# Linear attention ahead of two feed-forward stages: q, k, v laid out with token groups on partitions, and conversions re-timed

## The chip, the cores and the metric

The kernel runs on one core of a Trainium2 chip. The metric is the device time of one execution in microseconds (us). The engines are TensorE (PE in the profile; PEld is its weight load), VectorE (DVE), ScalarE (ACT), GpSimd (POOL) and SyncE (SP), which issues the transfers; the core's 16 DMA engines move the data.

## What is computed

```python
kv  = einsum('bhsd,bhse->bhde', k, v)            # 4 batches, 8 heads, 576 tokens, head size 64
out = einsum('bhsd,bhde->bhse', q, kv)
x   = out / sqrt(mean(out**2) + 1e-6) * g_norm   # then as 2304 tokens x 512
h   = x @ w_in;  g = h * clip(h + 3, 0, 6) / 6   # 512 -> 2048
x   = g @ w_out                                  # 2048 -> 512
out = sum over 4 experts of p_e * (relu(x @ w1[e]) @ w2[e])
```

All inputs and outputs are float32. The large products are made from a high and a low part of each factor (`xH`, `xL`, `gH`, `gL`, and `w[:, h, 0]`, `w[:, h, 1]` for the weights), three products for one.

## The kernel before

**Three stretches.** The attention fills roughly the first 73 us, the first feed-forward (`step`, `ff_in`, `ff_out`) comes next, and the four experts (`quad`, `outs`) take the rest. The change lies in the attention and in what is woven into it; the order of instructions on PE, DVE and ACT behind the attention is the same in both kernels.

**The attention's items.** There are `NHB` = 8 items: one batch and half of its heads, that is `HH` = 4 heads of 576 tokens. `att_load(i)` loads q, k and v of item i, 576 KB each. A head's tokens are numbered s*9 + j with 64 values of s and 9 of j (`CP` = 64, `CJ` = 9). Before, the partition is (head's parity x, s): one load fills all 128 partitions, and each partition gets runs of 9*64 floats, 2304 bytes. `att_q` transposes q on PE and ACT copies it out of PSUM, `att_kv` sums k-transposed times v over the 9 values of j (36 matmuls over 64 rows each), `att_out` multiplies q by that, `att_rms` forms the norm on DVE and ACT, and `att_x` transposes the result and writes its high and low part.

**Order.** In the attention the order on PE, DVE and ACT is the order in which the code stands (`manual_schedule`). Step i of the loop runs `att_load(i + 2)`, `att_out(i)`, `att_q(i + 1)`, `att_rms(i)`, `att_kv(i + 1)`, one half of a first feed-forward product (`ff_mm` at even i, `ff_in(..., later=True)` at odd i, from i = 2), `att_x(i - 1)` and then `conv(SLOTS[i])`. Tiles for two items exist, so the loads of item i + 2 reuse those of item i, and wait until PE has read them. SP issues all loads, one after the other.

**Weights of the first feed-forward.** `load_raw` loads one raw half tile (512 KB): h = 0 is a piece of `w_in`, h = 1 one of `w_out`; there are three buffers. `convert` is a generator that turns it into the two parts on ACT, DVE and for the first three half tiles GpSimd (L161, L164); each `next` is a slot, mostly one DVE instruction. `conv(k)` runs k slots. A finished half tile calls `load_raw` for the next.

**Low part of an item's product.** `ff_in` forms `gL` = r - `gH` on DVE (L360).

Of the kernel before, what the change touches and what calls it, by code (L numbers as in the profile page):

```python
# [17 lines left out]
def kernel(  # L18
# [28 lines left out]
    CP = P // 2  # L47
    CJ = S // CP
    CB = TB // CP
    HH = H // 2  # L50
    NP = HH // 2
# [30 lines left out]
    psa = ctx.enter_context(tc.tile_pool(name="psa", bufs=1, space=bass.MemoryType.PSUM))  # L82
# [4 lines left out]
    psx = attps.enter_context(tc.tile_pool(name="psx", bufs=1, space=bass.MemoryType.PSUM))  # L87
# [9 lines left out]
    ident = const.tile([P, P], F32, name="ident")  # L97
# [3 lines left out]
    dp = const.tile([P, B, CJ, E], F32, name="dp")  # L101
# [71 lines left out]
    st = {}  # L173
    natile = [0]

    def att_load(i):
# [12 lines left out]


    half = [slice(x * D, (x + 1) * D) for x in range(2)]
    identx = ident.rearrange("p (x s) -> p x s", x=2)
    GB = TB // D
    ppA = psp.tile([P, TB], F32, name="ppA")
    ppB = psp.tile([P, 2 * TB], F32, name="ppB")
# [1 line left out]
    def group(g):  # L197
        t, o = (ppA, g) if g < GB else (ppB, g - GB)
        return t[:, o * D:(o + 1) * D]
# [3 lines left out]
    def att_q(i):  # L203

        t = st[i]
        qT = wp.tile([P, (CJ + 1) * P], F32, tag=f"w{i % 2}", name="qT")
        t["qm"] = qm = qT[:, :2 * TB].rearrange("p (r x j s) -> p r x j s", r=NP, x=2, j=CJ // 2)
        t["q8"] = q8 = qT[:D, 2 * TB:].rearrange("p (r x s) -> p r x s", r=NP, x=2)
        pq = [pool.tile([P, 2, CJ // 2, CP], F32, tag=tag, name="pq") for pool, tag in ((psx, "x"), (psa, "a1"))]
        t["kvp"] = kvp = psk.tile([P, NP, TB], F32, tag="k", name="kvp")  # L210
        p8 = kvp[:D, :, D:D + P].rearrange("p r (x s) -> p r x s", x=2)
        for r in range(NP):
            for j in range(CJ // 2):
                nc.tensor.transpose(  # L214
                    pq[r][:, :, j, :], t["q"][:, r, 2 * j:2 * j + 2, :].rearrange("p j d -> p (j d)"), identx)
            nc.tensor.transpose(p8[:, r], t["q"][:, r, CJ - 1, :], identx)
        return [
            lambda r=r: nc.scalar.activation(
                out=qm[:, r].rearrange("p x j s -> p (x j s)"), in_=pq[r].rearrange("p x j s -> p (x j s)"),
                func=AF.Copy)  # L220
            for r in range(NP)] + [
            lambda: nc.scalar.activation(
                out=q8.rearrange("p r x s -> p r (x s)"), in_=kvp[:D, :, D:D + P], func=AF.Copy)]

    def att_kv(i):


        t = st[i]
        kvp = t["kvp"]
        for j in range(CJ):  # L230
            for x in range(2):
                for r in range(NP):
                    nc.tensor.matmul(  # L233
                        kvp[half[x ^ r], r, :D], lhsT=t["k"][half[x], r, j, :], rhs=t["v"][half[x], r, j, :],
                        start=(j == 0), stop=(j == CJ - 1))
        nc.scalar.activation(out=kvd[i % 2][:, 0], in_=kvp[:, :, :D], func=AF.Copy)
        for y in range(2):
            nc.scalar.activation(out=kvd[i % 2][half[y], 1], in_=kvp[half[1 - y], :, :D], func=AF.Copy)

    GA = CJ - 1  # L240

    def att_out(i):

        t = st[i]
        kv = kvd[i % 2]
        for jj in range(CJ // 4):
            for r in range(NP):
                for x in range(2):
                    for y, c in ((0, 0), (1, 1), (0, 1), (1, 0)):
                        g = (2 * y + jj) * HH + 2 * r + x  # L250
                        nc.tensor.matmul(
                            group(g)[half[c]], lhsT=t["qm"][half[y], r, x, 2 * jj + c, :],
                            rhs=kv[half[y], x ^ r ^ y, r], start=True, stop=True)
        for x in range(2):
            for r in range(NP):
                g = 2 * GA + x
                nc.tensor.matmul(
                    group(g)[half[r]], lhsT=t["q8"][:, r, x, :], rhs=kv[half[0], x ^ r, r],
                    start=True, stop=True)
# [87 lines left out]
    def ff_in(u, t, f, later=False, cs=(0, 1, 2, 3)):  # L347
        n = BLK[t][1]
        ff_mm(u, t, f, cs)
        ph = ph_t.pop((u, t, f))  # L350
        gH = gp.tile([P, TB], F32R, tag="gH", name="gH")[:, :n]
        gL = gp.tile([P, TB], F32R, tag="gL", name="gL")[:, :n]
        r = rp.tile([P, TB], F32, tag="r", name="r")[:, :n]
        gt[u, t, f] = gH, gL
        parts = [
            lambda: nc.scalar.activation(out=r, in_=ph, func=AF.Relu, bias=three[:, 0:1]),  # L356
            lambda: nc.vector.scalar_tensor_tensor(  # L357
                out=r, in0=r, scalar=6.0, in1=ph, op0=ALU.min, op1=ALU.mult),
            lambda: nc.scalar.activation(out=gH, in_=r, func=AF.Copy),
            lambda: nc.vector.tensor_tensor(out=gL, in0=r, in1=gH.bitcast(F32), op=ALU.subtract),  # L360
        ]
        if later:
            return parts
        for x in parts:
            x()
# [56 lines left out]
    start = {}  # L422
# [51 lines left out]

    nc.scalar.activation(out=gcol, in_=three, func=AF.Sqrt)
    att_load(1)
    load_raw()
    nc.sync.dma_start(out=gcol[0:D, :], in_=g_norm.rearrange("(p o) -> p o", o=1))
    nc.sync.dma_start(out=gcol[D:2 * D, :], in_=g_norm.rearrange("(p o) -> p o", o=1))
    SLOTS = {0: 8, 1: 2, 2: 3, 3: 0, 4: 3, 5: 1, 6: 3, 7: 0}  # L480
    nop = lambda: None
    engines = {mybir.EngineType.PE, mybir.EngineType.Activation, mybir.EngineType.DVE}
    with tc.manual_schedule(engines=engines):
# [97 lines left out]
        for y in range(2):  # L581
            h = half[y]
            for jp in range(2):
                j = slice(2 * y + jp, CJ - 1, 4)
                nc.vector.tensor_tensor(
                    out=prob[h, :B * HH].rearrange("p (b a) e -> p b a e", b=B)[:, :, 2 * jp:2 * jp + 2],
                    in0=dp[h, :, j], in1=psum_e[h, :, j].unsqueeze(3).to_broadcast([D, B, 2, E]), op=ALU.mult)
            nc.vector.tensor_tensor(
                out=prob[h, B * HH:], in0=dp[h, y::2, CJ - 1],
                in1=psum_e[h, y::2, CJ - 1:].to_broadcast([D, 2, E]), op=ALU.mult)  # L590

    N3 = start[NU1 - 1, 0] + 3 * UF[NU1 - 1]
    for n in range(NB, N3 + 1):
# [147 lines left out]
    def finish(p, e, i, ps):  # L741
        n = rows[p][i]
        pe = prob[:, n, e:e + 1]
        if e == 0:
            z = (p * NI2 + i) % 10
            acc2[i] = gp.tile([P, TB], F32, tag=("gH", "gL")[z % 2], name="acc2") if z < 8 else rp.tile(
                [P, TB], F32, tag="r", name="acc2")
            nc.vector.tensor_scalar(out=acc2[i], in0=ps, scalar1=pe, scalar2=None, op0=ALU.mult)
        else:
            nc.vector.scalar_tensor_tensor(  # L750
                out=acc2[i], in0=ps, scalar=pe, in1=acc2[i], op0=ALU.mult, op1=ALU.add)
        if e == E - 1:
            for y in range(2):
                if n < B * HH:
                    b, a = divmod(n, HH)
                    j = 4 * (a % 2) + a // 2 + 2 * y
                else:
                    b, j = 2 * (n - B * HH) + y, CJ - 1
# [141 lines left out]
```

## Time and profile before

| | |
|---|---|
| median of 3 runs | 1217.32 us (1217.02 to 1217.51) |
| profiled execution | 1218.32 us |
| its span on the core | 1216.5 us |
| PE busy | 1195.3 us, 98% |
| DVE, ACT, POOL busy | 770.1, 581.7, 8.9 us |
| DMA, mean over the span | 72 GB/s |

A span is the time from the core's first to its last instruction; the execution lasts 1.8 us longer. Shares over the whole span say little about the attention, which is 6% of it, so that stretch has to be read by itself. Of an instruction the profile gives its start, its duration, and what ended the idle time before it. The DMA share is the part of the 16 engines' time in which they had a packet in hand.

### The profile page before, as it was taken

The numbers are of one execution on the slowest core, as the hardware profiler recorded it, in microseconds if no ns is written. First come the engines' busy times: TensorE is split into PE (matmuls) and PEld (weight loads), VectorE is DVE, ScalarE is ACT, GpSimd is POOL, SyncE is SP. The second block draws the span as 40 slices with busy tenths as digits, with TensorE's granted clock in tenths as the row PEclk, the third lists the DMA queues.
The fourth block names the chain that finished last, engine by engine and source line by source line (L and its number), as shares of the span: only waits on it lengthen the run. The fifth ranks groups of instructions, "written<-read, shape, count | busy, mean of one in ns | idle before, by whom it ended". The sixth has DMA issues, their size and how long they took to land.

```text
span 1216.5 us, 17419 instructions
## 1 busy us (share of the span) xinstructions
PE 1195.3 (98%) x6999; PEld 1053.8 (87%) x6999; DVE 770.1 (63%) x1455; ACT 581.7 (48%) x1116; POOL 8.9 (1%) x16
## 2 busy tenths in 40 slices
PE   7899999999999999999999999999999999999997
PEld 6787888888888889999999989999999899999996
DVE  5889999953633844565656585656565856565652
ACT  5766554622322434444444554444445644444441
POOL 2000000000000000000000000000000000000000
PEclk9999999999999999999999999999999999999999
DMA  9612222300200002121111131122221422222202
GB/s 354 223 36 70 87 87 70 95 10 1 70 1 1 1 20 84 70 70 69 69 61 61 62 113 70 70 70 70 70 70 70 121 70 70 70 70 70 70 1 52
DMA packets 59345, 87.18 MB, mean 72 GB/s; under 512 B 3712, under 2 KB 36480, under 8 KB 59264
## 3 DMA queue, kind: packets, MB, share of 16 engines
q1 hardware_dynamic: 59264, 86.07, 21.1%
q8 instruction: 55, 0.90, 0.3%
q14 instruction: 26, 0.21, 0.0%
HBM read 81.34 MB, written 4.72 MB: 71 GB/s over the span
## 4 chain that ended last, share of the span: by engine, by line
PE 93%; DVE 3%; DMA 2%; ACT 1%; issue 1%; SPq 0%; DVEq 0%; ACTq 0%
PE po L734 32%; PE po L378 15%; PE qa L767 14%; PE qb L767 14%; PE ph L343 5%; PE ph L344 5%; PE ph L345 5%; DMA vin<-in_v_dram 1%; DMA qin<-in_q_dram 1%; DVE acc L750 1%; DVE xl L301 1%; PE kvp L233 1%; DVE r L357 0%; PE pq L214 0%; DVE ssq L264 0%
## 5 line engine op out<-in xcount | busy, mean ns | idle before, releaser
L734 PE MATMUL po<-wout,g 128*128 128x512 f32 x1728 | 402.1, 390 | 0.0
L734 PEld LDWEIGHTS po<-wout,g 128*128 128x128 f32 x1728 | 323.6, 188 | 65.4
L767 PE MATMUL qb<-xs,win 128*128 128x384 f32 x1008 | 203.5, 336 | 1.2 <-ACT us L808 1.2
L767 PE MATMUL qa<-xs,win 128*128 128x384 f32 x1008 | 203.1, 336 | 0.0
L378 PE MATMUL po<-gH,w 128*128 128x512 f32 (+1 forms) x632 | 191.8, 368 | 0.0
L767 PEld LDWEIGHTS qb<-xs,win 128*128 128x128 f32 x1008 | 178.1, 188 | 3.8 <-ACT us L808 1.8
L767 PEld LDWEIGHTS qa<-xs,win 128*128 128x128 f32 x1008 | 178.3, 188 | 2.2 <-ACT us L808 0.2
L641 DVE TENSOR_TENSOR wout<-raw,wout 128x512 fp32r<-128x512 f32 x96 | 62.2, 688 | 171.4 <-ACT wout L640 171.4
L640 ACT ACTIVATE wout<-raw 128x512 fp32r<-128x512 f32 x96 | 55.4, 625 | 227.0 <-PE po L734 227.0
L378 PEld LDWEIGHTS po<-gH,w 128*128 128x128 f32 x632 | 115.7, 188 | 20.5 <-ACT acc L392 0.6
L343 PE MATMUL ph<-xh,w 128*128 128x512 f32 (+1 forms) x320 | 119.2, 373 | 1.2 <-DVE r L357 1.2
L344 PE MATMUL ph<-xl,w 128*128 128x512 f32 (+1 forms) x320 | 118.4, 370 | 0.0
L345 PE MATMUL ph<-xh,w 128*128 128x512 f32 (+1 forms) x320 | 118.2, 370 | 0.0
L356 ACT ACTIVATE r<-ph,three 128x512 f32<-128x512 f32 (+1 forms) x80 | 51.6, 645 | 138.3 <-PE ph L345 138.2
L378 PE MATMUL po<-gL,w 128*128 128x512 f32 (+1 forms) x316 | 116.3, 368 | 0.0
L357 DVE SCALAR_TENSOR_TENSOR r<-r,ph 128x512 f32<-128x512 f32 (+1 forms) x80 | 50.5, 631 | 91.0 <-ACT r L356 90.8
L797 DVE SCALAR_TENSOR_TENSOR g<-sums,g 128x384 fp32r<-128x384 f32 x96 | 53.6, 559 | 81.4 <-ACT g L794 81.4
L794 ACT ACTIVATE g<-cs 128x384 fp32r<-128x384 f32 x96 | 50.4, 525 | 63.3 <-DVE cs L810 54.4
L640 ACT ACTIVATE win<-sums 128x512 fp32r<-128x512 f32 x96 | 60.6, 632 | 40.1 <-DVE sums L653 37.6
L343 PEld LDWEIGHTS ph<-xh,w 128*128 128x128 f32 x320 | 60.6, 189 | 12.4 <-DVE r L357 1.6
L797 DVE SCALAR_TENSOR_TENSOR g<-cs,g 128x384 fp32r<-128x384 f32 x96 | 53.2, 554 | 27.2 <-ACT g L794 27.2
L345 PEld LDWEIGHTS ph<-xh,w 128*128 128x128 f32 x320 | 60.6, 189 | 10.3
(129 smaller groups left out, 1260.7 us busy)
## 6 DMA issues: line engine op xcount, KB each, us to landing
raw<-in_moe_w_dram SPq DMA_DIRECT2D x96, 512.0 KB, 4.1
raw<-in_moe_w_in_dram SPq DMA_DIRECT2D x16, 512.0 KB, 3.7
raw<-in_moe_w_out_dram SPq DMA_DIRECT2D x16, 512.0 KB, 3.5
qin<-in_q_dram SPq DMA_DIRECT2D x8, 576.0 KB, 7.1
kin<-in_k_dram SPq DMA_DIRECT2D x8, 576.0 KB, 8.3
vin<-in_v_dram SPq DMA_DIRECT2D x8, 576.0 KB, 9.4
out_dram<-acc SPq DMA_DIRECT2D x36, 128.0 KB, 2.3
dp<-in_moe_domain_probs_dram SPq DMA_DIRECT2D x2, 36.0 KB, 8.4
```

The source lines that it names most:

```text
L343: nc.tensor.matmul(ph, lhsT=w[:, 0, c, :], rhs=xH[t][:, c, :], start=(c == 0), stop=False)
L344: nc.tensor.matmul(ph, lhsT=w[:, 0, c, :], rhs=xL[t][:, c, :], start=False, stop=False)
L345: nc.tensor.matmul(ph, lhsT=w[:, 1, c, :], rhs=xH[t][:, c, :], start=False, stop=(c == KD - 1))
L356: lambda: nc.scalar.activation(out=r, in_=ph, func=AF.Relu, bias=three[:, 0:1]),
L357: lambda: nc.vector.scalar_tensor_tensor(out=r, in0=r, scalar=6.0, in1=ph, op0=ALU.min, op1=ALU.mult),
L378: nc.tensor.matmul(po_t[u, t][o], lhsT=lhsT, rhs=rhs, start=(f == 0 and m == 0), stop=(f == UF[u] - 1 and m == 2))
L640: nc.scalar.activation(out=dst[0], in_=src, func=AF.Copy)
L641: nc.vector.tensor_tensor(out=dst[1], in0=src, in1=dst[0].bitcast(F32), op=ALU.subtract)
L734: nc.tensor.matmul(ps[i], lhsT=lhsT, rhs=w[:, f, y], start=(j == 0 and f == 0 and m == 0), stop=(j == FP - 1 and f == 1 and m == 2))
L767: nc.tensor.matmul(bank, lhsT=w[:, wy, AOP[m], c], rhs=xs[m][:, xy, c], start=first and n == 0, stop=n == 5, skip_group_check=True)
L794: nc.scalar.activation(out=g[f][:, 0, t], in_=src, func=func)
L797: nc.vector.scalar_tensor_tensor(out=g[f][:, 1, t], in0=src, scalar=0.0, in1=g[f][:, 0, t].bitcast(F32), op0=ALU.max, op1=ALU.subtract)
```

## The change

**Layout.** The partition is now (token group y, s): group 0 holds j = 0 to 4, group 1 holds j = 5 to 8, and each of the four heads has its own place in the row. One tensor of an item comes in two loads, one per group, each into 64 partitions, with runs of 1280 and 1024 bytes. `att_kv` then sums over 128 rows for four values of j and over 64 rows for the fifth: 20 matmuls for 36. `att_q` has 12 transposes for 10, `att_out` has as many matmuls as before. `att_q`, `att_out`, the routing weights `prob` and the rows that `finish` stores only follow the new numbering.

**Raw loads and slots.** The `load_raw` ahead of the loop is gone, and the calls in the loop are at i = 0, 3 and 5 for i = 1 and 3. `SLOTS` has the same sum, 20, with fewer slots early and more in steps 2 to 6.

**Low part.** `ff_in(..., later=True)` forms `gL` on GpSimd; that is three instructions of 80.

```diff
     def att_load(i):
...
-            t[nm] = pool.tile([P, NP, CJ, D], F32, tag=tag, name=f"{nm}in")
-            nc.sync.dma_start(
-                out=t[nm].rearrange("p r j d -> p r (j d)"),
-                in_=src[b, hf * HH:(hf + 1) * HH].rearrange("(r x) (s j) d -> (x s) r (j d)", x=2, j=CJ),
-            )
+            t[nm] = pool.tile([P, HH, JG, D], F32, tag=tag, name=f"{nm}in")
+            for y in range(2):
+                j = slice(y * JG, min((y + 1) * JG, CJ))
+                nc.sync.dma_start(
+                    out=t[nm][half[y], :, :j.stop - j.start].rearrange("p h j d -> p h (j d)"),
+                    in_=src[b, hf * HH:(hf + 1) * HH].rearrange("h (s j) d -> s h j d", j=CJ)[:, :, j]
+                    .rearrange("s h j d -> s h (j d)"))
...
     def att_kv(i):
...
-        for j in range(CJ):
-            for x in range(2):
-                for r in range(NP):
+        for j in range(JG):
+            rows = slice(0, P) if j < JP else half[0]
+            for r in range(NP):
+                for x in range(2):
                     nc.tensor.matmul(
-                        kvp[half[x ^ r], r, :D], lhsT=t["k"][half[x], r, j, :], rhs=t["v"][half[x], r, j, :],
-                        start=(j == 0), stop=(j == CJ - 1))
+                        kvp[half[x], r, :D], lhsT=t["k"][rows, 2 * r + x, j, :], rhs=t["v"][rows, 2 * r + x, j, :],
+                        start=(j == 0), stop=(j == JP))
...
-            lambda: nc.vector.tensor_tensor(out=gL, in0=r, in1=gH.bitcast(F32), op=ALU.subtract),
+            lambda: (nc.gpsimd if later else nc.vector).tensor_tensor(out=gL, in0=r, in1=gH.bitcast(F32), op=ALU.subtract),
...
     att_load(1)
-    load_raw()
...
-    SLOTS = {0: 8, 1: 2, 2: 3, 3: 0, 4: 3, 5: 1, 6: 3, 7: 0}
+    SLOTS = {0: 2, 1: 0, 2: 4, 3: 2, 4: 5, 5: 3, 6: 4, 7: 0}
...
-            if i in (1, 3):
+            if i in (0, 3, 5):
                 load_raw()
```

`JG` is 5, `JP` is 4, and `half[y]` is the upper or lower 64 partitions.

On SP, the kernel's first loads before (items 0 and 1 and the first two raw half tiles, by name of the tile and tensor, with partitions x runs x floats of a run):

```order
L184 DMA qin<-in_q_dram 128x2x576
L184 DMA kin<-in_k_dram 128x2x576
L184 DMA vin<-in_v_dram 128x2x576
L126 DMA raw<-in_moe_w_in_dram 128x4x256
L184 DMA qin<-in_q_dram 128x2x576
L184 DMA kin<-in_k_dram 128x2x576
L184 DMA vin<-in_v_dram 128x2x576
L130 DMA raw<-in_moe_w_out_dram 128x1024
```

and the start of the same place with the change:

```order
L190 DMA qin<-in_q_dram 64x4x320
L190 DMA qin<-in_q_dram 64x4x256
L190 DMA kin<-in_k_dram 64x4x320
L190 DMA kin<-in_k_dram 64x4x256
L190 DMA vin<-in_v_dram 64x4x320
L190 DMA vin<-in_v_dram 64x4x256
L126 DMA raw<-in_moe_w_in_dram 128x4x256
L190 DMA qin<-in_q_dram 64x4x320
L190 DMA qin<-in_q_dram 64x4x256
```

Each load is now two, of 64 partitions each, and the raw `w_out` tile stands no longer behind item 1 but behind item 2.

On SP, the last loads of the attention with the change (end of item 6, a raw `w_out` tile, item 7, the next raw `w_in` tile):

```order
L190 DMA vin<-in_v_dram 64x4x320
L190 DMA vin<-in_v_dram 64x4x256
L130 DMA raw<-in_moe_w_out_dram 128x1024
L190 DMA qin<-in_q_dram 64x4x320
L190 DMA qin<-in_q_dram 64x4x256
L190 DMA kin<-in_k_dram 64x4x320
L190 DMA kin<-in_k_dram 64x4x256
L190 DMA vin<-in_v_dram 64x4x320
L190 DMA vin<-in_v_dram 64x4x256
L126 DMA raw<-in_moe_w_in_dram 128x4x256
```

Ahead of item 7 stand four raw tiles in all; before there were five, all of them ahead of item 6.

On DVE, between the products of the low parts `xl` of steps 3 and 4 before (`gL` is the low part of an item, `ssq` the sums of squares):

```order
L301 SCALAR_TENSOR_TENSOR xl_123<-px,gcol,xh_118 128x512 x2
L301 SCALAR_TENSOR_TENSOR xl_126<-kvp,gcol,xh_121 128x2x64
L360 TENSOR_TENSOR gL<-r,gH 128x512
L264 TENSOR_REDUCE ssq<-xt 128x8
L264 TENSOR_REDUCE ssq<-xt 128x10
```

and with the change:

```order
L306 SCALAR_TENSOR_TENSOR xl_123<-px,gcol,xh_118 128x512 x2
L306 SCALAR_TENSOR_TENSOR xl_126<-kvp,gcol,xh_121 128x2x64
L158 TENSOR_SCALAR x<-a 128x512
L269 TENSOR_REDUCE ssq<-xt 128x8
L269 TENSOR_REDUCE ssq<-xt 128x10
```

The `gL` is gone from DVE, and a slot of a conversion stands in its place; steps 4 and 5 get two further slots each.

## Rows read from the trace of the kernel before

**Rows 1.** The page's 40 equal slices of the span.

```profile
DMA  9612222300200002121111131122221422222202
GB/s 354 223 36 70 87 87 70 95 10 1 70 1 1 1 20 84 70 70 69 69 61 61 62 113 70 70 70 70 70 70 70 121 70 70 70 70 70 70 1 52
```

**Rows 2.** Busy time by stretch: PE, PEld, DVE, ACT, POOL, granted clock, DMA share, GB/s.

```profile
2.00:22.00 20.00, 16.34 (x343) 13.14 (x345) 9.70 (x20) 10.54 (x26) 3.78 (x3) 1.00 1.01 369
22.00:42.00 20.00, 14.84 (x408) 12.50 (x409) 15.05 (x34) 13.27 (x32) 1.30 (x2) 0.97 0.92 329
42.00:58.00 16.00, 15.93 (x351) 13.35 (x349) 12.40 (x27) 11.60 (x29) 2.56 (x2) 0.93 0.70 220
58.00:76.00 18.00, 16.97 (x292) 14.14 (x291) 16.93 (x35) 14.98 (x31) 0.00 (x0) 1.00 0.01 2
76.00:100.00 24.00, 22.81 (x109) 18.14 (x109) 19.18 (x38) 16.95 (x33) 0.00 (x0) 1.00 0.22 67
```

**Rows 3.** The chain of waits, 0 to 130 us: start, duration, what.

```profile
10.95 10.83 DMA vin<-in_v_dram
21.91 1.31 PE kvp L233 x72
...
37.68 2.89 issue
...
61.94 1.21 PE kvp L233 x72
...
73.91 1.39 PE po L546 x6
```

**Rows 4.** PE's timeline around item 7: start, duration, instruction, what ended idle time.

```profile
61.09 0.30 PE L216 MATMUL kvp<-ident,qin 128*64 128x128 f32 x1 [0.20 <-DVE xl L301]
...
61.87 1.28 PE L233 MATMUL kvp<-vin,kin 64*64 64x64 f32 x72
```

**Rows 5.** SP's issues in the attention: the first, and item 7's last.

```profile
0.73 0.44 SPq L184 DMA_DIRECT2D qin<-in_q_dram  x1
...
49.65 0.46 SPq L184 DMA_DIRECT2D vin<-in_v_dram  x1
```

**Rows 6.** The page's transfers: issue, count, KB each, us to landing.

```profile
raw<-in_moe_w_in_dram SPq DMA_DIRECT2D x16, 512.0 KB, 3.7
...
dp<-in_moe_domain_probs_dram SPq DMA_DIRECT2D x2, 36.0 KB, 8.4
```

**Rows 7.** Transfers from 18 to 22 us, nearly all q, k, v.

```profile
DMA packets 744, 1.62 MB, mean 405 GB/s; under 512 B 47, under 2 KB 47, under 8 KB 743
```

**Rows 8.** Transfers from 7 to 8 us, nearly all runs of 1 KB.

```profile
DMA packets 327, 0.34 MB, mean 339 GB/s; under 512 B 6, under 2 KB 319, under 8 KB 327
```

**Rows 9.** Transfers from 1206 to 1216 us: the last stores, of 64 partitions each.

```profile
DMA packets 960, 1.57 MB, mean 157 GB/s; under 512 B 192, under 2 KB 192, under 8 KB 960
...
q1 hardware_dynamic: 960, 1.57, 67.6%
...
out_dram<-acc SPq DMA_DIRECT2D x12, 128.0 KB, 2.3
```

**Rows 10.** Busy time inside the stretch of the stores, columns as in rows 2.

```profile
1208.00:1214.00 6.00, 1.01 (x5) 0.51 (x3) 1.80 (x3) 0.00 (x0) 0.00 (x0) 0.80 0.88 205
```

**Rows 11.** Busy time around the stretch at half clock, columns as in rows 2.

```profile
35.00:40.80 5.80, 2.91 (x103) 2.56 (x95) 5.37 (x13) 3.33 (x7) 0.00 (x0) 1.00 0.92 306
40.80:44.20 3.40, 3.40 (x22) 2.60 (x15) 0.00 (x0) 1.37 (x5) 0.00 (x0) 0.50 0.62 179
```

**Rows 12.** DVE's timeline, steps 3 to 4.

```profile
46.97 0.68 DVE L360 TENSOR_TENSOR gL<-r,gH 128x512 fp32r<-128x512 f32 x1
...
53.56 0.68 DVE L155 SCALAR_TENSOR_TENSOR a<-raw,x 128x512 uint32<-128x512 uint32 x1
54.27 0.43 DVE L158 TENSOR_SCALAR x<-a 128x512 uint32<-128x512 uint32 x1
```

**Rows 13.** GpSimd's timeline, one conversion.

```profile
54.84 1.27 POOL L161 TENSOR_TENSOR r<-r,x 128x512 f32<-128x512 f32 x1 [31.46 <-ACT qT L218]
```

More of the change, by code (lines that the diff above doesn't have):

```diff
@@ L174 @@
     natile = [0]
+    JG, JP = CJ // 2 + 1, CJ // 2
+    half = [slice(x * D, (x + 1) * D) for x in range(2)]
     def att_load(i):
@@ L182, in att_load @@
             pool, tag = (accp, "acc") if m < 5 else (wp, f"w{m - 1}")
-            t[nm] = pool.tile([P, NP, CJ, D], F32, tag=tag, name=f"{nm}in")
-            nc.sync.dma_start(
-                out=t[nm].rearrange("p r j d -> p r (j d)"),
-                in_=src[b, hf * HH:(hf + 1) * HH].rearrange("(r x) (s j) d -> (x s) r (j d)", x=2, j=CJ),
-            )
+            t[nm] = pool.tile([P, HH, JG, D], F32, tag=tag, name=f"{nm}in")
[5 more added lines that the diff above has]
+                    .rearrange("s h j d -> s h (j d)"))
         st[i] = t
-    half = [slice(x * D, (x + 1) * D) for x in range(2)]
-    identx = ident.rearrange("p (x s) -> p x s", x=2)
     GB = TB // D
@@ L206, in att_q @@
         qT = wp.tile([P, (CJ + 1) * P], F32, tag=f"w{i % 2}", name="qT")
-        t["qm"] = qm = qT[:, :2 * TB].rearrange("p (r x j s) -> p r x j s", r=NP, x=2, j=CJ // 2)
-        t["q8"] = q8 = qT[:D, 2 * TB:].rearrange("p (r x s) -> p r x s", r=NP, x=2)
-        pq = [pool.tile([P, 2, CJ // 2, CP], F32, tag=tag, name="pq") for pool, tag in ((psx, "x"), (psa, "a1"))]
+        t["qm"] = qm = qT[:, :2 * TB].rearrange("p (h j t) -> p h j t", h=HH, j=JP // 2)
+        t["q8"] = q8 = qT[:D, 2 * TB:].rearrange("p (h s) -> p h s", h=HH)
+        pq = [pool.tile([P, 2, JP // 2, P], F32, tag=tag, name="pq") for pool, tag in ((psx, "x"), (psa, "a1"))]
         t["kvp"] = kvp = psk.tile([P, NP, TB], F32, tag="k", name="kvp")
         p8 = kvp[:D, :, D:D + P].rearrange("p r (x s) -> p r x s", x=2)
-        for r in range(NP):
-            for j in range(CJ // 2):
+        for h in range(HH):
+            r, x = divmod(h, 2)
+            for j in range(JP // 2):
                 nc.tensor.transpose(
-                    pq[r][:, :, j, :], t["q"][:, r, 2 * j:2 * j + 2, :].rearrange("p j d -> p (j d)"), identx)
-            nc.tensor.transpose(p8[:, r], t["q"][:, r, CJ - 1, :], identx)
+                    pq[r][:, x, j, :], t["q"][:, h, 2 * j:2 * j + 2, :].rearrange("p j d -> p (j d)"), ident)
+            nc.tensor.transpose(p8[:, r, x], t["q"][half[0], h, JP, :], ident[half[0], :D])
         return [
             lambda r=r: nc.scalar.activation(
-                out=qm[:, r].rearrange("p x j s -> p (x j s)"), in_=pq[r].rearrange("p x j s -> p (x j s)"),
-                func=AF.Copy)
+                out=qm[:, 2 * r:2 * r + 2].rearrange("p x j t -> p (x j t)"),
+                in_=pq[r].rearrange("p x j t -> p (x j t)"), func=AF.Copy)
             for r in range(NP)] + [
             lambda: nc.scalar.activation(
-                out=q8.rearrange("p r x s -> p r (x s)"), in_=kvp[:D, :, D:D + P], func=AF.Copy)]
+                out=q8.rearrange("p (r x) s -> p r (x s)", x=2), in_=kvp[:D, :, D:D + P], func=AF.Copy)]
     def att_kv(i):
@@ L245, in att_out @@
         kv = kvd[i % 2]
-        for jj in range(CJ // 4):
+        for jj in range(JP // 2):
             for r in range(NP):
@@ L249, in att_out @@
                     for y, c in ((0, 0), (1, 1), (0, 1), (1, 0)):
-                        g = (2 * y + jj) * HH + 2 * r + x
                         nc.tensor.matmul(
-                            group(g)[half[c]], lhsT=t["qm"][half[y], r, x, 2 * jj + c, :],
-                            rhs=kv[half[y], x ^ r ^ y, r], start=True, stop=True)
+                            group((2 * y + jj) * HH + 2 * r + x)[half[c]],
+                            lhsT=t["qm"][half[y], 2 * r + x, jj, half[c]],
+                            rhs=kv[half[y], x ^ y, r], start=True, stop=True)
         for x in range(2):
             for r in range(NP):
-                g = 2 * GA + x
                 nc.tensor.matmul(
-                    group(g)[half[r]], lhsT=t["q8"][:, r, x, :], rhs=kv[half[0], x ^ r, r],
+                    group(2 * GA + x)[half[r]], lhsT=t["q8"][:, 2 * r + x, :], rhs=kv[half[0], x, r],
                     start=True, stop=True)
@@ L583 @@
             for jp in range(2):
-                j = slice(2 * y + jp, CJ - 1, 4)
+                j = slice(JG * y + jp, JG * y + JP, 2)
                 nc.vector.tensor_tensor(
-                    out=prob[h, :B * HH].rearrange("p (b a) e -> p b a e", b=B)[:, :, 2 * jp:2 * jp + 2],
+                    out=prob[h, :B * HH].rearrange("p (b z a) e -> p b z a e", b=B, z=2)[:, :, jp],
                     in0=dp[h, :, j], in1=psum_e[h, :, j].unsqueeze(3).to_broadcast([D, B, 2, E]), op=ALU.mult)
             nc.vector.tensor_tensor(
-                out=prob[h, B * HH:], in0=dp[h, y::2, CJ - 1],
-                in1=psum_e[h, y::2, CJ - 1:].to_broadcast([D, 2, E]), op=ALU.mult)
+                out=prob[h, B * HH:], in0=dp[h, y::2, JP],
+                in1=psum_e[h, y::2, JP:JP + 1].to_broadcast([D, 2, E]), op=ALU.mult)
     N3 = start[NU1 - 1, 0] + 3 * UF[NU1 - 1]
@@ L755, in finish @@
                     b, a = divmod(n, HH)
-                    j = 4 * (a % 2) + a // 2 + 2 * y
+                    j = 2 * (a % 2) + a // 2 + JG * y
                 else:
-                    b, j = 2 * (n - B * HH) + y, CJ - 1
+                    b, j = 2 * (n - B * HH) + y, JP
                 nc.sync.dma_start(
```

1 line of the change is left out of this document (removed).

## The prediction, made before the run

> **What bounds the kernel now.** I read the slices of the page first: behind the third slice the transfers need a small part of the time, while in the first two the 16 DMA engines are busy for nearly all of it [rows 1]. So the busy time by stretch comes next, for the attention alone. From 2 to 22 us the engines have a packet in hand all the time and PE's 16.34 us hold much filling work; from 22 to 42 us it is still 0.92; from 58 us on nothing is loaded and DVE is busy for 16.93 of 18 us [rows 2]. The reader is to see two regimes: loads set the pace at first, the chain through PE, ACT and DVE later. The chain of waits says the same: 10.83 us of it are v of the third item, which ends in that item's kv product [rows 3]. Late, PE reaches item 7's q and kv work after a wait for DVE [rows 4], and item 7's last load had been issued at 49.65 us [rows 5], 12 us ahead. Behind item 7's kv product (its end at 61.94 + 1.21 = 63.15 us) the same instructions follow in both kernels but for one `gL`, so the end moves with that moment. That is the quantity to forecast.
>
> **The loads, part by part.** An item is 3 x 576 KB = 1.77 MB. Now it runs at 405 GB/s [rows 7], 4.37 us per item. The change alters two things.
>
> Shorter runs: runs of 1 KB go at 339 GB/s [rows 8], those of 2304 bytes at 405. Per engine (a sixteenth) that is 48.3 ns for 1024 bytes and 91.0 ns for 2304; a straight line between them gives 56.9 ns for 1280. A pair of new runs takes 105.2 ns for the 91.0 of an old one: 5.05 us per item, 0.68 more.
>
> 64 partitions per load: the only loads of that kind in the trace are small (the routing weights, 36 KB in runs of 144 bytes [rows 6]) and tell nothing of pace, but the stores of the result are of that kind too. The last twelve, 128 KB each, alternate between the two halves exactly as the new loads would, and move 205 GB/s while the engines hold packets for 0.88 of the time [rows 10]. Their packets are long: 67.6% of 16 x 10 us are 108 us, over 768 packets of 2 KB (the 192 short ones left at nothing) 141 ns each [rows 9], where the line above gives 82 ns. Engines that are busy and still slow share something, and following a load of the lower half by one of the upper did not free it. I carry this over to the loads. The bounds are 205 GB/s and 205/0.88 = 233 GB/s, if the gaps could be filled at the same pace; I take 212, since an engine's gap is also when another runs faster, so filled gaps give less than their share.
>
> [...]
>
> **The sum.** Eight items at 212 GB/s are 8 x 8.34 = 66.7 us. Four raw half tiles lie ahead of item 7's last piece, one behind item 0: two of 1 KB runs (524 KB at 339 GB/s = 1.55 us) and two of longer ones (at 405, 1.30 us), 5.7 us. A lone raw tile lands after 3.7 us [rows 6], 1.55 of them moving, so 2.2 us are latency. The first issue is at 0.73 us [rows 5]. Item 7's v then lands at 0.73 + 2.2 + 66.7 + 5.7 = 75.3 us, if the queue never empties: k and v of item i + 2 wait for PE's reading of item i, and item i + 1 (8.3 us of transfer) is then still on its way. SP issues twice as often, six loads of some 0.46 us [rows 5] in those 8.3 us, so it keeps up. It lets eight loads be under way and waits for the first of them before the ninth; with loads half as large these are 8 x 288 KB = 2.4 MB, 11 us at the forecast's pace, so that wait too leaves the engines with work.
>
> The kv product after it: 40 matmul passes instead of 72. In 1.21 us [rows 3] 72 of 64 rows went in four quarters of the array. If the rate of issue is the limit, 40 take 0.67 us; if twice as many rows take twice as long, 1.34. I take 1.0. It ends at 76.3 us, 13.2 later than before.
>
> [...] With 8.3 us per item PE idles more, so the same can meet the products behind item 7: nothing to 1.7 us for one such stretch, 2 us as the bound; I take 1.0. The sum is 14.2 us later: 1218.3 + 14.2 = 1232.5 us for the profiled execution. That execution is 1.0 us above the median of the runs, so the median comes out at **1231.5 us**.
>
> **What lies under this.** The transposes (12 for 10), the moved slots and the low part cost nothing here: each step waits some 8.3 us for its loads, and the steps before needed about 7 (42 to 63 us for three). Without that cover, three slots more in steps 4 and 5 are two DVE instructions of 0.43 and one of 0.68 us [rows 12], and others on ACT; against them stand two `gL` of 0.68 us [rows 12] off DVE, which take GpSimd 1.27 us each by its nearest row [rows 13]. Nothing waits for those in the same step. The third `gL` lies in the last step, and its reader stands behind another product of the first feed-forward; cover again. The raw `w_out` tile's new place is worth 1.3 us for item 2 and nothing at item 7, where the total counts; there one raw tile fewer stands ahead, and it is in the sum.
>
> **The rivals.** *Faster: the stores' pace is a matter of stores.* If loads into 64 partitions only pay for shorter runs, items 0 to 2 land 3 x 0.68 = 2.0 us later, less 1.3 for the `w_out` tile; from item 3 on kv is up to 0.54 us shorter per item, 2.7 in all, and 1.4 us of `gL` leave DVE's chain against 0.9 us of slots: 0.7 - 2.7 - 0.5 = -2.5, so 1214.8 us. PE's unexplained pause in the middle of a kv product, 2.89 us [rows 3], may shrink with fewer instructions: down to 1211.9. For it: stores end in DRAM, loads don't. Against it: the engines' packets were held up, not the queue. [...]
>
> *Same: gain and loss cancel.* As above, but kv stays near 1.21 us (twice the rows, half the count) and the `gL` had been in DVE's idle time: 0.7 + 0.9 - 0.7 = about +1, at most 1219.
>
> *Slower by little: conversions.* Loads at full pace and a DVE that carries the extra slots of steps 4 to 6 (0.9 us), ACT with two more copies of one 128x512 tile at 0.65 us (DVE's row for that size is 0.68 [rows 12]), the first items later by 0.7, kv and `gL` without a gain: 0.9 + 1.3 + 0.7 = 2.9, 1220.2 us. It decides if DVE, not the loads, ends the waits in steps 4 and 5, and if `gL` had stood in idle time.
>
> **How the numbers follow.** The forecast's own range: at 233 GB/s the items take 60.7 us, with kv at 0.67 and no half clock 1224.2; at 205, with kv at 1.34 and 2 us of clock, 1235.2, and one more for a queue that empties now and then, 1236. It gets 0.78, the faster rival 0.12, the same 0.05, the small loss 0.05. A measurement of this kernel tells 0.2%, 2.4 us, from no change. Faster by more: 0.12, since most of that rival's spread lies at or below 1214.9. Same: 0.05. Slower: 0.78 and the small loss of 2.9 us: 0.83. The range 1220 to 1237 leaves out the fast cases and little else.
>
> **What would show it.** Right: transfers of q, k, v at 200 to 235 GB/s with the engines busy, until beyond 70 us; PE's waits in every step end with v's load; item 7's kv product ends near 76 us. Wrong: those loads near 350 GB/s, or the steps from 42 us on still waiting for DVE. If loads run at 350 GB/s, the forecast falls as a whole.

## The result, and the profile of the changed kernel

The changed kernel takes 1230.84 us (median of 4 runs, 1229.60 to 1231.11), the kernel before on the same chip 1217.41 us (median of 4 runs): a ratio of 1.0105, 95% interval 1.0088 to 1.0123, so 13.4 us slower. The forecast was 1231.5 us. The profiled execution spans 1229.3 us, 12.8 more than before.

The page of the changed kernel, its 40 slices:

```profile
PEclk8999999999999999999999999999999999999999
DMA  9942222210100001221111142212112321112102
GB/s 222 240 109 70 86 70 85 91 47 1 58 11 1 1 1 69 69 70 69 69 69 70 69 120 69 69 69 69 69 69 69 93 97 69 69 69 69 69 1 52
```

Against [rows 1] the first two slices, 354 and 223 GB/s before, now move 222 and 240, and the third, 36 before, moves 109: much the same bytes, later. The engines are as full as before: a share of 1.07 and 1.10 in the first two stretches, for 1.01 and 0.92. The stretches of [rows 2] for the changed kernel (the columns are the same; the number before the last is the DMA share, the sum of the packets' times over that of 16 engines, which comes to 1.10 here):

```profile
2.00:22.00 20.00, 16.13 (x190) 11.10 (x188) 5.69 (x13) 6.19 (x15) 2.53 (x2) 0.83 1.07 234
22.00:42.00 20.00, 16.75 (x271) 12.51 (x268) 10.31 (x23) 10.26 (x25) 0.00 (x0) 0.84 1.10 241
42.00:58.00 16.00, 14.56 (x269) 11.14 (x267) 12.67 (x28) 11.55 (x26) 3.80 (x3) 0.98 1.10 236
58.00:76.00 18.00, 16.09 (x287) 12.37 (x287) 14.28 (x29) 12.99 (x29) 3.46 (x3) 1.00 1.00 231
76.00:100.00 24.00, 22.82 (x189) 18.93 (x188) 18.66 (x36) 17.02 (x34) 1.64 (x2) 1.00 0.08 26
```

The engines have a packet in hand throughout, up to 73 us instead of about 54, at 231 to 241 GB/s where before it was 369 and 329. DVE has 5.69 us of work in the first 20, for 9.70 before: it is starved (e1 below, with the old slots, has 5.80). Where the loads end can be seen in two short stretches:

```profile
70.00:73.00 3.00, 2.57 (x80) 1.88 (x75) 3.00 (x5) 2.93 (x7) 1.27 (x1) 1.00 0.97 204
73.00:74.00 1.00, 1.00 (x12) 0.62 (x11) 0.96 (x3) 0.30 (x1) 0.27 (x1) 1.00 0.31 71
```

Item 7's last load, the second one of v, is issued at 63.1 us and lands 10.0 us later, at 73.1. A raw tile and the routing weights move beside it and behind it.

The chain of waits, which answers to [rows 3]:

```profile
8.69 10.63 DMA vin<-in_v_dram
19.33 8.47 DMA vin<-in_v_dram
27.82 10.80 DMA vin<-in_v_dram
38.76 2.36 PE kvp L239 x40
...
48.14 1.46 PE kvp L239 x40
...
70.34 1.61 DVE xl L306 x3
72.00 0.24 PE kvp L221
72.24 0.37 PE pq L219 x2
...
73.86 0.38 PE kvp L239 x7
74.24 0.42 issue
74.66 1.35 PE kvp L239 x33
...
87.24 1.39 PE po L550 x6
```

Two regimes again, but the border has moved: up to item 3 the chain is one load of v after the other; from item 4 on it runs through DVE's `xl`, PE's transposes and the kv product, with v there first. Item 7's kv product ends at 74.66 + 1.35 = 76.01 us, 12.9 later than before, and the first product of the routed output (`po`) begins at 87.24 for 73.91: 13.3 us. Behind it the kernels run alike, and the last half microsecond of that is regained by the end.

A compact way to follow the attention is the moment at which ACT begins to copy each item's kv product out (`kvd<-kvp`, the copy of 128x128), read from ACT's timeline of each kernel:

```
                              item 0     1      2      3      4      5      6      7
before                          9.29  16.13  23.25  31.40  41.17  49.70  56.75  63.69
changed                        13.95  22.14  30.71  41.17  49.79  58.68  67.36  76.06
before, loads of 64 (e1)       12.37  23.58  32.55  45.04  57.81  66.61  73.65  80.93
changed, loads of 128 (e3)     10.24  16.29  23.61  30.69  38.66  46.53  54.41  62.78
e3, transposes grouped (e8)     9.91  15.96  22.47  29.09  37.06  44.22  51.80  59.67
tokens on 128 (e11)            11.27  18.36  24.75  32.17  40.15  47.73  55.23  63.58
e11, tiles in their places     10.94  17.37  23.53  30.02  38.02  45.17  52.50  60.37
```

The changed kernel is 9.8 us behind by item 3, and loses 2.6 more in the four steps after it (34.9 us for 32.3).

### The profile page after: what moved, and what is told of

The parts are those of the page before. It is cut to its first block, busy times and chain, and to the rows that moved or that the text cites. A ratio compares the mean times of both kernels' runs of the same rounds, so it can differ in the third digit from the quotient of the medians.

```text
span 1229.3 us, 16977 instructions
## 1 busy us (share of the span) xinstructions
PE 1206.4 (98%) x6759; PEld 1057.4 (86%) x6759; DVE 769.3 (63%) x1452; ACT 582.1 (47%) x1116; POOL 12.7 (1%) x19
## 4 chain that ended last, share of the span: by engine, by line
PE 92%; DMA 3%; DVE 2%; ACT 1%; issue 0%; SPq 0%; DVEq 0%
PE po L738 31%; PE po L383 15%; PE qa L771 14%; PE qb L771 14%; PE ph L348 5%; PE ph L349 5%; PE ph L350 5%; DMA vin<-in_v_dram 2%; PE kvp L239 1%; DVE acc L754 1%; DVE xl L306 1%; DMA kin<-in_k_dram 0%; PE pq L219 0%; DMA raw<-in_moe_w_out_dram 0%; PE kvp L221 0%
```

## Experiments

The theory: loads of 64 partitions move at some 235 GB/s whatever else is done, and that makes the loss. The rivals: the number of loads, the short runs, the new layout's other work (transposes, DVE, GpSimd), the re-timed conversions.

**e1: only the partitions, on the kernel before.** Each load of q, k and v is cut into two of 64 partitions, with its runs of 2304 bytes.

```diff
+            for y in range(2):
+                nc.sync.dma_start(
+                    out=t[nm][y * D:(y + 1) * D].rearrange("p r j d -> p r (j d)"),
+                    in_=src[b, hf * HH:(hf + 1) * HH].rearrange("(r x) (s j) d -> x s r (j d)", x=2, j=CJ)[y])
```

> The kernel before, each q, k, v load cut in two by partition: 64 partitions each, runs of 2304 bytes as they were; nothing else changes. Theory (a load into 64 partitions moves at about half pace): transfers at 200 to 240 GB/s with the engines busy up to about 70 us, and 1228 to 1232 us. Rival, short runs cost the time: no run is shorter, so 1217 us within 1. Rival, the number of loads (twice the issues and completions, eight under way): 1228 to 1231 us as well. Rival, the changed kernel's own PE and DVE work: 1217 us within 1.

Measured: 1234.83 us against 1218.26, ratio 1.0140 (1.0125 to 1.0155), 16.6 us slower. Its stretches, 2 to 22 and 22 to 42 us:

```profile
2.00:22.00 20.00, 13.56 (x206) 10.21 (x208) 5.80 (x13) 6.16 (x15) 2.53 (x2) 0.97 1.03 251
22.00:42.00 20.00, 14.28 (x306) 11.71 (x299) 9.81 (x20) 9.79 (x23) 2.54 (x2) 0.76 1.06 243
```

The long runs of before at nearly the pace of the changed kernel, with engines as full. One thing was changed, and it costs more than the whole change. The time lies above the 1228 to 1232 us expected; why it costs so much more was not tried. PE's granted clock from 42 to 58 us is 0.82 in e1 and 0.98 in the changed kernel, which may be a part of it.

**e2: only the number of loads, on the kernel before.** Two loads of 128 partitions, one for each pair of heads.

```diff
+            for y in range(2):
+                nc.sync.dma_start(
+                    out=t[nm].rearrange("p r j d -> p r (j d)")[:, y],
+                    in_=src[b, hf * HH:(hf + 1) * HH].rearrange("(r x) (s j) d -> (x s) r (j d)", x=2, j=CJ)[:, y])
```

> The kernel before, each q, k, v load cut in two by pair of heads: 128 partitions each, one run of 2304 bytes per partition, as many loads and as many bytes per load as in the run of two loads with 64 partitions. Theory (64 partitions): back near 400 GB/s, 1217 us, at most 1219. Rival, short runs: 1217 us. Rival, the number of loads: 1228 to 1231 us. Rival, PE and DVE work: 1217 us.

Measured: 1217.30 us, ratio 0.9999 (0.9989 to 1.0009). Twice as many loads cost nothing.

**e3: the changed kernel with one load of 128 partitions**, and **e4: with two, whose runs are as short as the changed kernel's.**

The first diff is e3's, the second e4's.

```diff
-            for y in range(2):
-                j = slice(y * JG, min((y + 1) * JG, CJ))
...
+            nc.sync.dma_start(
+                out=t[nm].rearrange("p h j d -> p (h j d)").rearrange("p (r z) -> p r z", r=NP)[:, :, :CJ * D],
+                in_=src[b, hf * HH:(hf + 1) * HH].rearrange("(r x) (s j) d -> (x s) r (j d)", x=2, j=CJ))
...
```

```diff
...
+                    out=t[nm].rearrange("p h j d -> p (h j d)").rearrange("p (r z) -> p r z", r=NP)[:, :, j.start * D:j.stop * D],
+                    in_=src[b, hf * HH:(hf + 1) * HH].rearrange("(r x) (s j) d -> (x s) r j d", x=2, j=CJ)[:, :, j]
+                    .rearrange("p r j d -> p r (j d)"))
...
```

> The changed kernel, its loads replaced by those of before: one per tensor, 128 partitions, runs of 2304 bytes, same bytes in all; the data lands at other tokens' places and for two of the four heads the ninth token value of k, v and q is taken from the neighbouring head, so that the computation differs while its instructions stay the same. Theory (64 partitions): the loads stop bounding; what is left is the changed kernel's longer chain in the late steps (8.7 us a step against 7.0 in its profile, part of it waiting for loads): 1216 to 1221 us. Rival, short runs: the same. Rival, PE and DVE work of the changed kernel makes the loss: 1228 to 1231 us.

> The changed kernel with two loads per tensor of 128 partitions and two heads each, in place of 64 partitions and four heads: same count of loads, same bytes per load, same runs of 1280 and 1024 bytes; data and the ninth value as in the run with one load. Theory (64 partitions): transfers near 350 GB/s, 0 to 2 us above the run with one load, 1216 to 1223 us. Rival, short runs: 1228 to 1231 us. Rival, number of loads: 1228 to 1231 us. Rival, PE and DVE work: 1228 to 1231 us.

Measured: e3 1218.07 us, ratio 1.0003 (0.9993 to 1.0012); e4 1217.93, 1.0004 (0.9995 to 1.0014). The stretch of 2 to 22 us of e3, then of e4:

```profile
2.00:22.00 20.00, 19.45 (x280) 13.35 (x278) 7.93 (x17) 9.67 (x24) 2.55 (x2) 1.00 0.97 365
```

```profile
2.00:22.00 20.00, 19.46 (x278) 13.41 (x276) 7.55 (x16) 9.46 (x23) 2.56 (x2) 1.00 1.04 364
```

With 128 partitions the loads are back at 365 GB/s and the loss is gone, with short runs as with long ones; e1 and e3 together show the cause from both sides. Runs of 1280 and 1024 bytes instead of 2304 raise the share (0.97 to 1.04), not the time. In the traces e4's items come 0.5 us later than e3's, from the first (ACT's copy at 10.73 for 10.24 us) to the last (63.23 for 62.78): once, and not 0.68 us for each of the first three, as the prediction had priced the shorter runs.

**e5: the layout without the new times** (the old slots, the raw `w_out` tile and `gL` as before), and **e6: the new times without the layout** (the kernel before with the changed kernel's three). The diff is e5's; e6's is the same the other way about.

```diff
-    SLOTS = {0: 2, 1: 0, 2: 4, 3: 2, 4: 5, 5: 3, 6: 4, 7: 0}
+    SLOTS = {0: 8, 1: 2, 2: 3, 3: 0, 4: 3, 5: 1, 6: 3, 7: 0}
...
-            lambda: (nc.gpsimd if later else nc.vector).tensor_tensor(out=gL, in0=r, in1=gH.bitcast(F32), op=ALU.subtract),
+            lambda: nc.vector.tensor_tensor(out=gL, in0=r, in1=gH.bitcast(F32), op=ALU.subtract),
...
-            if i in (0, 3, 5):
+            if i in (1, 3):
```

> The changed kernel with the old times: slots, raw loads and the low part on DVE as before, so the layout and its loads of 64 partitions alone. Theory (loads bound; five raw tiles lie ahead of item 7's last piece where the change has four): one raw tile more, 1.3 us, and slots and low part under cover: 1231 to 1233 us, against 1230.8 for the whole change. Rival, the moved slots and the low part are worth some us in a kernel bound by loads: 1234 to 1236 us.

> The kernel before with the moved slots and raw loads and with the low part on GpSimd, but with its own layout and loads of 128 partitions. Theory (late steps wait for PE and DVE in turn, gain and loss of these moves about cancel): 1216 to 1219 us. Rival, the moves help on their own: at or below 1215 us. Rival, they hurt, as GpSimd's operation holds a DVE instruction up (in the changed kernel's profile one of 0.68 us took 1.33 beside it) and late steps carry more slots: 1219 to 1221 us.

Measured: e5 1233.53 us, ratio 1.0129 (1.0116 to 1.0143), just above the range expected; e6 1217.93, 0.9998 (0.9989 to 1.0007). The times alone do nothing measurable. With the layout, the change is some 2 us better than e5 (13.4 for 15.4 us over their own runs of before), though the intervals overlap by a little: where loads set the pace, one raw tile fewer ahead of the last item can be time. No run moves the raw tile alone, so this is not shown.

**e7: the second half's loads from another queue.** Two queues, so that a load into the lower and one into the upper half can be under way at once.

```diff
-                nc.sync.dma_start(
+                (nc.sync if y == 0 else nc.gpsimd).dma_start(
```

> The changed kernel with the loads of the second token group issued from GpSimd's queue, those of the first from SP's, so that loads into the lower and the upper 64 partitions are under way together. If what is short is a path into one half of the partitions, and the 16 engines take packets of both queues in turn: up to 300 GB/s and more, 1219 to 1226 us. If the engines themselves are slow with such loads, in whatever order: 230 to 250 GB/s, 1229 to 1232 us. GpSimd's own issue may cost more than SP's and hold up its other work: then above 1232 us.

Measured: 1235.62 us, ratio 1.0154 (1.0138 to 1.0170). Its stretches of 2 to 22 and 42 to 58 us:

```profile
2.00:22.00 20.00, 17.52 (x191) 11.61 (x190) 3.92 (x9) 6.16 (x16) 7.11 (x15) 1.00 1.03 262
...
42.00:58.00 16.00, 13.32 (x204) 10.51 (x206) 10.38 (x23) 9.47 (x23) 3.73 (x6) 0.89 1.09 234
```

12% more at the start, nothing later, with GpSimd now issuing loads between waits. Both queues were at work together: from 42 to 58 us the packets of SP's queue took 69.0% of the engines' time and those of GpSimd's 38.5%. The order in which one queue hands out the halves is not what holds the pace.

**e8: e3 with its transposes in another order.** In e3 (and in the changed kernel) three transposes stand in turn for each head, two of 128 rows and one of 64. Here the eight large ones of a step come first, then the four small ones.

```diff
                     pq[r][:, x, j, :], t["q"][:, h, 2 * j:2 * j + 2, :].rearrange("p j d -> p (j d)"), ident)
+        for h in range(HH):
+            r, x = divmod(h, 2)
             nc.tensor.transpose(p8[:, r, x], t["q"][half[0], 2 * r, JP, :], ident[half[0], :D])
```

> The run of the changed kernel with one load of 128 partitions, with the eight transposes of 128 rows first and the four of 64 rows behind them, in place of two and one in turn (the computation differs as in that run). Theory on the longer late steps: the small ones wait for DVE, the large ones queue behind them, and each change of size costs: 2.1 us a step falls to 1.2, four to five steps are shortened by 0.5 to 0.9 each: 2 to 4 us less than with one load alone (1218.1), 1214 to 1216 us. Rival, DVE alone bounds the late steps: no difference, 1217 to 1219 us.

Measured: 1214.28 us, ratio 0.9971 (0.9962 to 0.9981): 3.8 us below its own runs of before, where e3 was level with them. PE's timeline of e3 (one head's pair and the small one behind it), then that of e8 (a whole step, and its kv product):

```profile
59.07 0.24 PE L218 MATMUL kvp<-ident,qin 64*64 64x64 f32 x1 [0.43 <-DVE xl L303]
59.24 0.44 PE L216 MATMUL pq<-ident,qin 128*128 128x128 f32 x2
59.61 0.24 PE L218 MATMUL kvp<-ident,qin 64*64 64x64 f32 x1
```

```profile
55.28 1.26 PE L216 MATMUL pq<-ident,qin 128*128 128x128 f32 x8
56.48 0.41 PE L220 MATMUL kvp<-ident,qin 64*64 64x64 f32 x4
56.81 1.53 PE L238 MATMUL kvp<-vin,kin 128*64 128x64 f32 x40
```

In turn a head takes 0.54 us (59.07 to 59.61), 2.16 a step; grouped, a step takes 1.53 (55.28 to 56.81). And only the small ones write the tile that waits for DVE's `xl`: grouped, the large ones go ahead of that wait. The two gains were not told apart, and they are not the late steps' alone: of the 3.1 us by which e8 leads e3 at item 7 in the table, 1.6 are there at item 3.

**e9: the same grouping in the kernel before.**

```diff
                     pq[r][:, :, j, :], t["q"][:, r, 2 * j:2 * j + 2, :].rearrange("p j d -> p (j d)"), identx)
+        for r in range(NP):
             nc.tensor.transpose(p8[:, r], t["q"][:, r, CJ - 1, :], identx)
```

> The kernel before with the eight large transposes of an item first and the two small ones behind them; nothing else. Theory on the late steps: PE's wait for DVE then holds up only the small ones; the second four large ones, 0.44 us, leave the chain of each of items 4 to 7: 1 to 2 us less than before, 1216 to 1217 us beside 1218. Rival, DVE alone bounds the late steps: no difference beyond 0.5 us.

Measured: 1217.12 us, ratio 0.9996 (0.9988 to 1.0005). A miss: the 1 to 2 us expected are not there. The kernel before has two such transposes in a step, not four, and grouping them gains nothing that can be measured.

**e10: e8 with `gL` back on DVE.**

```diff
-            lambda: (nc.gpsimd if later else nc.vector).tensor_tensor(out=gL, in0=r, in1=gH.bitcast(F32), op=ALU.subtract),
+            lambda: nc.vector.tensor_tensor(out=gL, in0=r, in1=gH.bitcast(F32), op=ALU.subtract),
```

> The changed kernel with one load of 128 partitions and grouped transposes, with the low part of an item back on DVE (the computation differs as in the run with one load). If GpSimd's operation, which holds a DVE slot up by 0.65 us twice, gives back what it takes off DVE (0.6 us twice): within 0.5 us of that run (1214.3). If the hold-up is the greater cost: up to 1 us less. If the low part on DVE is: 1 to 1.5 us more.

Measured: 1214.82 us, ratio 0.9983 (0.9970 to 0.9995); its interval overlaps that of e8. Where `gL` is computed can't be told apart in the time. A cost of a microsecond for DVE is not excluded either: in the traces item 7's copy comes at 60.91 us here and at 59.67 in e8.

**e11: the idea of the layout without its loads.** Tokens 4p to 4p + 3 of an item go to partition p, on all 128, by one load with runs of 1 KB; the last 64 tokens come by a small load of 64 partitions; transposes grouped, and the result stored by 128 partitions, but for the last 64 tokens of each batch.

```diff
-    dp = const.tile([P, B, CJ, E], F32, name="dp")
-    psum_e = const.tile([P, B, CJ], F32, name="psum_e")
+    dp = const.tile([P, B, CJ // 2 + 1, E], F32, name="dp")
+    psum_e = const.tile([P, B, CJ // 2 + 1], F32, name="psum_e")
...
+            nc.sync.dma_start(
+                out=t[nm][:, :, :JP].rearrange("p h j d -> p h (j d)"),
+                in_=src[b, hf * HH:(hf + 1) * HH, :JP * P].rearrange("h (p j) d -> p h (j d)", j=JP))
+            nc.sync.dma_start(
+                out=t[nm][half[0], :, JP], in_=src[b, hf * HH:(hf + 1) * HH, JP * P:].rearrange("h s d -> s h d"))
...
+                    out=out[b * S:b * S + JP * P].rearrange("(p j) d -> j p d", j=JP)[j], in_=acc2[i])
```

> The changed kernel with another numbering of tokens: partition p holds tokens 4p to 4p + 3 of the first 512, which one load of 128 partitions brings in runs of 1 KB, and 64 partitions the last 64 tokens in a small load of 64 KB; transposes grouped; the results of 512 tokens are stored 128 partitions at a time. Computes what the reference does. Theory: loads near 350 GB/s, so the front is that of the run with one load and grouped transposes (1214.3) or up to 1 us later for short runs; the stores at the end, 8 for 12 of which four have 128 partitions and full pace, end 1 to 3 us earlier: 1211 to 1214 us. Rival, the small loads of 64 partitions bound the items after all: 1220 us or more.

Measured: 1226.00 us, ratio 1.0068 (1.0055 to 1.0081). A miss by over 12 us, and not in the attention: its item 7 is where it was before (table above). Its loads at 22 to 42 us, and its groups of matmuls, by form:

```profile
22.00:42.00 20.00, 17.17 (x332) 13.94 (x331) 15.88 (x36) 14.20 (x35) 0.00 (x0) 1.00 1.12 294
```

```profile
L775 PE MATMUL qb<-xs,win 128*128 128x384 f32 x1008 | 205.7, 338 | 1.2 <-ACT us L816 1.2
...
L384 PE MATMUL po<-gH,w 128*128 128x512 f32 x504 | 169.2, 396 | 0.0
L349 PE MATMUL ph<-xh,w 128*128 128x512 f32 x256 | 102.1, 399 | 1.9 <-DVE r L363 1.1 <-ACT qT L224 0.7
```

The next run's expectation tells what was read from this: matmuls a little slower each, in feed-forward stages that the edit had not touched. Not all of them are: the largest group (`po<-wout,g`, 1728 matmuls) has 389 ns here and 390 in the kernel before. The chip is not the reason, since e9 and e10, on the same one, have 390 ns for `po<-gH,w`. What the edit had touched is the size of two small tiles, and so the place of every tile allocated behind them: 4 batches x 4 tokens x 5 numbers x 4 bytes = 320 bytes.

**e12: e11 with every tile back in its place.**

```diff
-    dp = const.tile([P, B, CJ // 2 + 1, E], F32, name="dp")
+    dp = const.tile([P, B, CJ, E], F32, name="dp")[:, :, :CJ // 2 + 1]
-    psum_e = const.tile([P, B, CJ // 2 + 1], F32, name="psum_e")
+    psum_e = const.tile([P, B, CJ], F32, name="psum_e")[:, :, :CJ // 2 + 1]
```

> The kernel of the run before (tokens 4p to 4p+3 on 128 partitions, the last 64 tokens by a small load), whose attention was as early as that of the kernel before (item 7's k x v product ended at 63.6 us, and the output rows began at the same time) but which then fell behind steadily, by 8 us between 120 and 450 us and by 0.25 us in each 100 us after that, its 512-column matmuls at 393 to 399 ns where the kernel before has 389 to 395. Here the two tiles that it had shrunk, those of the domain probabilities and of their sums, get back their allocated size (only their first five columns are used), so that every tile behind them lies 320 bytes further on in each partition, where it lies in the kernel before. The instructions are the same, one by one. Theory A, the matmuls' operands had been shifted to places from which they are read more slowly: the 512-column matmuls return to 389 to 395 ns, there is no drift, and the time is that of the kernel before less what the late steps' grouped transposes and the end's stores give, 1217.5 - 0 to 4 = 1213.5 to 1217.5. Theory B, the drift has to do with the order of the data or of the program (the values on the partitions, where instruction loads fall): the time stays at 1225 to 1227, and the mean of the 512-column matmuls stays high.

Measured: 1212.55 us, ratio 0.9956 (0.9944 to 0.9969). The same stretch and groups:

```profile
22.00:42.00 20.00, 19.14 (x405) 15.94 (x405) 17.39 (x39) 16.05 (x39) 0.44 (x1) 1.00 1.10 336
```

```profile
L775 PE MATMUL qb<-xs,win 128*128 128x384 f32 x1008 | 203.2, 336 | 1.2 <-ACT us L816 1.2
...
L384 PE MATMUL po<-gH,w 128*128 128x512 f32 x504 | 166.2, 390 | 0.0
L349 PE MATMUL ph<-xh,w 128*128 128x512 f32 x256 | 100.7, 393 | 1.2 <-DVE r L363 1.2
```

Places decide: 320 bytes were worth 13 us, in the matmuls (399 to 393 ns, 396 to 390) and also in the loads (294 to 336 GB/s), with the same instructions: theory A. Of the 13.6 us between the two spans 3.2 are there at item 7 (63.58 for 60.37). The time is a microsecond below the range expected. Which of the shifted tiles matters, and why, was not tried. The change itself is free of this: the means of `po<-gH,w` and `qb<-xs,win` are 390 and 336 ns in the kernel before and in the changed one. This kernel is 5.1 us faster than the kernel before and 18 us faster than the changed one: it keeps the tokens on the partitions, and gives up only the bulk of the loads of 64. Of the 5.9 us between the profiled spans (1210.6 for 1216.5) 3.3 are there at item 7 (60.37 for 63.69), and 2.4 at the end: behind DVE's last `acc` the span goes on for 4.3 us (4.4 in e11), and for 6.8 in e3 and e8, 6.7 before, which store 64 partitions at a time. Whether the end gains by the partitions or by the smaller number of stores was not told apart.

## Why the prediction was right

**The mechanism** was the likeliest of those listed, and it holds: loads of 64 partitions are slow while the engines have packets in hand (231 to 241 GB/s at a share of 1.00 to 1.10, where e3's loads of 128 move 365 at 0.97). What they share was not shown. It was read from stores [rows 9, 10], and the carry from stores to loads, which the faster rival denied, is right: the last stores of the changed kernel move 205 GB/s at a share of 0.88 (1221 to 1227 us), 233 for full engines, and its loads much the same.

**The pace** was set at 212 GB/s, between 205 and 233. It was 231 to 241: the upper bound, gaps filled at the same pace, was nearly the true value, if a little low, and the reason for choosing below it (an engine's gap is when another runs faster) was wrong for loads that never run out. Over 8 items 66.7 us became about 14.16 MB / 236 GB/s = 60 us. The last v was forecast at 75.3 us and lands at 73.1: of those 6.7 us 4.5 are lost again elsewhere. A part of it are the raw tiles: at the shared pace they would take 2.1 MB / 236 GB/s = 8.9 us for 5.7, an estimate from above, since the first of them, from 11 to 12 us, moved at 360. Another is what moves beside the last v: it is a raw tile of 512 KB and the routing weights, which the sum left out. How much each took was not measured.

**Behind the landing** the sum had too little: the kv product was taken at 1.0 us (bounds 0.67 to 1.34) and has 1.46 for its 40 passes (the profile shows two for each matmul) where it runs through (item 4), more than the 1.21 of 72 passes in [rows 3]; with twice the rows a pass took somewhat more than twice as long here (1.46 us / 40 = 36.5 ns for 1.21 / 72 = 16.8). In item 7 it is 0.38 + 0.42 + 1.35 = 2.15, with a pause of 0.42 us. And 12 transposes instead of 10, "nothing, under cover", stand in the chain of each step from item 4 on, in item 7 with 1.86 us (72.00 to 73.86); before it was 0.85 there (61.09 to 61.94 [rows 3, 4]). They end 0.8 us behind v's landing. So the item's end came at 76.01 for 76.3: two terms, the landing too late by 2.2 and what follows it too short by 0.8 + 2.15 - 1.0 = 1.9, cancelled. The total is right; that it came so close is luck.

**One sign was wrong.** "PE's waits in every step end with v's load" holds up to item 3 only. From item 4 on the load is there first and the chain of DVE and PE ends the waits, though the transfers run on to 73 us. The cover for the transposes and the slots was therefore gone in the late half, where the prediction counted on 8.3 us of load against 7 of work. That cost is seen with the loads restored: e3, which has the change's transposes, comes out level with before, and e8, which groups them, 3.8 us below. In e3 the layout's gains and this cost cancel. The sum is that of the "same" rival, but not its mechanism: it had shorter runs and slots on the side of loss, not the transposes.

**The clock.** No run shows the 1.0 us that the sum puts in for half clock behind item 7; it was the author's estimate, from the 3.4 us at 0.50 in [rows 11]. In the changed kernel the granted clock from 58 to 100 us is 1.00, so the term is nothing there; it fell to 0.83 and 0.84 between 2 and 42 us, a mixture of stretches at 1.00 and at 0.50 (the latter from 8.4 to 15.2, 22.0 to 25.4 and 39.1 to 42.4 us), all in the items up to item 3, whose waits end with loads of v; item 3's kv product there took 2.36 us for the 1.46 of item 4 (granted clock 0.50 from 40 to 42 us). So half clock did stand on the chain, but at item 3, where the sum had none; the kernel before has such a stretch there too [rows 11], and what it makes of the difference was not tried.

**The rivals.** *Faster* needed loads at full pace: excluded by e1. With full pace (e3, e4) it did not come either, only with the transposes grouped as well (e8, 1214.28). *Slower by conversions* needed the slots to cost: e6 shows none. The prediction prices the moved slots at 0.43 + 0.43 + 0.68 = 1.5 us in one place and at 0.9 in the rivals; neither is in its forecast. The raw `w_out` tile's new place, "1.3 us for item 2" and one raw tile fewer ahead of item 7, is of the size of the 2 us between e5 and the change, which is no proof of it.

## What to carry to other kernels

Look at how many partitions a transfer spans before its run length or count: here two loads of 64 in place of one of 128 cost 16.6 us (e1), while doubling the number of loads (e2, ratio 0.9999) or cutting the runs in two (e4, 1217.93 us for e3's 1218.07) cost nothing that shows in the time. A layout that wants halves may be had with a transfer over all partitions for the bulk and a small one for the rest, as in e12 (1212.55 us). And when an edit changes the size of any tile, compare the mean duration of matmuls in stages that it did not touch: if they moved, the tiles' places may have done it, as in e11 (399 ns for 393, 396 for 390), and the edit is not measured until they are put back.

## What the runs showed beyond that

- **Places.** 320 bytes, as above: 13 us between e11 and e12.
- **Transposes in turn.** PE takes 0.54 us for a 64-row transpose and two of 128 rows in turn, 1.53 / 4 = 0.38 in groups (e3 and e8).
- **GpSimd beside DVE.** Two DVE operations that start beside GpSimd's `gL` take longer, 1.07 and 1.33 us. DVE's timeline of the changed kernel, then GpSimd's:

```profile
54.15 1.07 DVE L158 TENSOR_SCALAR x<-a 128x512 uint32<-128x512 uint32 x1
...
71.86 1.33 DVE L155 SCALAR_TENSOR_TENSOR a<-raw,x 128x512 uint32<-128x512 uint32 x1
```

```profile
53.67 1.27 POOL L365 TENSOR_TENSOR gL<-r,gH 128x512 fp32r<-128x512 f32 x1 [33.03 <-ACT gH L364]
...
71.37 1.27 POOL L365 TENSOR_TENSOR gL<-r,gH 128x512 fp32r<-128x512 f32 x1 [13.47 <-ACT gH L364]
```

The two take 0.43 and 0.68 us when alone [rows 12]. In both cases the DVE row ends 0.28 and 0.55 us behind GpSimd's end, somewhat less than the operation needs by itself. This gives back some 0.65 us of the 0.68 that a moved `gL` takes off DVE. e10, which can't be told from e8 in the time, leaves open what the whole is worth. What held the two up was not shown.
